# A second buffer for projected values, one key projection moved, reciprocals spread by four transfers, and another order of a store queue

## The chip, the cores and the metric

The kernel runs on 1 core of one Trainium2 chip. The metric is the device time of one execution in microseconds. A core has five engines with an instruction queue each: TensorE (PE in the profile: matmuls, with its weight loads as PEld), VectorE (DVE), ScalarE (ACT), GpSimd (POOL) and SyncE (SP). In this kernel POOL and SP compute next to nothing: POOL issues the loads, SP issues the transposing transfers, the spreads of reciprocals and the stores. Each queue is worked off in order.

## What is computed

For 8 batches, 8 heads, 1024 positions and 64 channels, attention with projected keys and values, and then a gated network over the 8192 tokens of 512 channels that come out of it:

```python
k_proj = np.einsum('ks,bhsd->bhkd', E, k)        # E, F: 64 x 1024
v_proj = np.einsum('ks,bhsd->bhkd', F, v)
scores = scale * np.matmul(q, k_proj.transpose(0, 1, 3, 2))
attn = softmax(scores)                            # over 64 projected positions
x = np.matmul(attn, v_proj)                       # rearranged to (8192, 512)
gate = 1.0 / (1.0 + np.exp(-(x @ w_gate)))        # 512 -> 1536
val = x @ w_val
out = (gate * val) @ w_out                        # 1536 -> 512
```

## The kernel before

**Work.** Matmuls are in bf16. The tokens are worked off in blocks of 512, two to a batch. A block has three units (K counts units, 3 to a block, 6 to a batch), each a third of the 1536 inner channels. The three big products are done as 2 x 2 block products with seven instead of eight multiplications: gate in `g_chain`, value in `v_chain` and output in `o_chain`; the sums of blocks that these need are made by DVE: `t_sums` (L1316, from wO to wT), `gt_sums` (from wG to gT), `xs_sums`, `s_sums`. The partial products go into PSUM banks pA0 to pA3 and pF0 to pF3, and ACT and DVE add them up, apply the sigmoid and evacuate them; `evac` (ACT, L1424) copies the output sums to the buffer ost, and SP stores them in `stored` (L1413), 4 stores of 256 KB a block. ost has four parts, and an evacuation waits for the stores that last read its parts (semaphores out0 to out3). A seed (L1653) puts a sum back into PSUM ahead of a product.

**Attention of the next batch** is interleaved with the units of the present one. In order of dependence:

- `load_k`, `load_v`, `load_q` (L395 to L430): POOL issues loads of 1 MB.
- `kv(b, bank)` (L863): 16 matmuls project keys and values into one bank. `keep_kd` (L879): ACT copies the keys to kpd, and SP issues the transfer that transposes them into kpD (L893). `vd_one` (L902): ACT copies the values into vpD, in two halves.
- `transpose_q` (L850): four transfers on SP from Qb to qT (L854).
- `sc_visit`: scores and their exponentials (eT), two visits of two rounds.
- `den_visit`: 16 matmuls with the patterns dsel8 (`den8`, L969) sum the denominators, DVE takes reciprocals (`rec`, L959) into rden; `spread` (L1126) stores rden to DRAM as rd (L1129) and reads it back with eight broadcasting transfers (L1146) into xu, seen as rb, four for each of two rounds.
- `xo_visit`: attention times values (from vpD) in a bank, and `scaled` (DVE, L1155 to L1159) multiplies it with rb into xT, the input of the next batch's gate and value products.

**Order.** The first 85 us or so are ordered by hand: a list of slots (`todo`) with pieces hung into them by `on` (L1876 to L1977). kv(2) is one of these pieces (`kv2`, L1962), together with t_sums and the transposes of q for batch 2. From there on a planner orders the work: the loop at L1997 hands it groups of matmuls with goals (times in a fictitious clock with 9.9 us per unit, PACE), and `arranged` (L52) simulates the five queues with the assumed costs in `COST` (L28; a transfer without a given time counts 3.0 us) and picks, whenever an engine is free, the ready entry with the least rank; ranks are derived backwards from goals. `Plan.add` (L146) records reads and writes by keys, and `emit` (L185) turns the result into one fixed program per engine with semaphore waits. So what the planner believes sets only the order within each queue; what an instruction really waits for follows from the keys and that order.

```python
pick = min((t for t in some if t.at <= first + 1e-9), key=lambda t: (t.rank, t.n))
...
self.busy, self.lat = (0.85 if eng == "POOL" else 0.6), t if t is not None else 3.0
```

In the loop, for a batch b the next batch's scores come in units late_ and late_+1 (late_ is 1 for b = 1, else 0), the denominators with the second of these, the first xo visit in unit late_+3, the second, and kv(b+2) after it, in unit late_+4.

Of the kernel before, what the change touches and what calls it, by code (L numbers as in the profile page):

```python
# [12 lines left out]
P = 128  # L13
# [17 lines left out]
class Task:  # L31
    def __init__(self, eng, call, t):
        self.eng, self.calls, self.goal = eng, [] if call is None else [call], None
        busy, tail = COST[eng]
        self.busy = busy if t is None else t
        self.lat = self.busy + tail
        self.dma = call is not None and call[5] is not None
        if self.dma:
            self.busy, self.lat = (0.85 if eng == "POOL" else 0.6), t if t is not None else 3.0
# [4 lines left out]
    def keys(self):  # L44
        r, w = set(), set()
        for c in self.calls:
            r.update(c[2])
            w.update(c[3] + c[4])
        return r - w, w, (r & w)


def arranged(tasks, free):  # L52
# [3 lines left out]
    for n, t in enumerate(tasks):  # L56
# [3 lines left out]
        def dep(o, raw):  # L60
# [4 lines left out]
            t.pre[o.n] = max(t.pre.get(o.n, 0.0), wait)  # L65
# [50 lines left out]
class Plan:  # L116
# [11 lines left out]
    def note(self, eng, call, t):  # L128
# [3 lines left out]
        else:  # L132
            self.tasks.append(Task(eng, call, t))

# [11 lines left out]
    def add(self, eng, fn, r=(), w=(), x=(), dma=None, t=None):  # L146
        if self.tasks is not None:
            self.note(eng, (eng, fn, tuple(r), tuple(w), tuple(x), dma), t)
            return None
# [80 lines left out]
def bass_linformer_attn__then__ffn_glu_sigmoid_kernel(  # L230
# [18 lines left out]
    with contextlib.ExitStack() as es:  # L249
# [11 lines left out]
        def within(shape, dtype):  # L261
# [24 lines left out]
        rhl = within([P, 256], BF16)  # L286
        quad = sbuf("quad", [P, 1], FP32)
        row_f = sbuf("row_f", [P, 1], FP32)
        rows = sbuf("rows", [P, 4, 32], FP32)
        half = sbuf("half", [P, 2], FP32)  # L290
        ident = sbuf("ident", [P, P], BF16)
# [10 lines left out]
        vpD = sbuf("vpD", [P, H, DH], BF16)  # L302
        qT = sbuf("qT", [P, H, 512], BF16)
        eT = sbuf("eT", [P, 8, 512], BF16)
        rden = sbuf("rden", [P, 256], FP32)
# [16 lines left out]
            "p (j h r c) -> p j h r c", j=4, h=2, r=2  # L322
        )

# [158 lines left out]

        def constants():
# [11 lines left out]
            for i, n in ((1, 8), (2, 4)):  # L496
                dve(
                    lambda e, i=i, n=n: e.tensor_copy(
                        pats[:, i, :].rearrange("p (a b) -> p a b", b=n),
                        count[:, 0:n].unsqueeze(1).to_broadcast([P, 32 // n, n]),  # L500
                    ),
                    ["count"],
                    ["pats"],
                )
# [41 lines left out]
            for t, k, m, w in ((dsel8, "dsel8", 8, 4),):  # L546
                for n in range(2):
                    for i in range(w):
                        dve(
                            lambda e, t=t, m=m, n=n, i=i: e.tensor_scalar(  # L550
                                t[:, n, i, :].rearrange("p (a b) -> p a b", b=m),
                                count[:, 0:m].unsqueeze(1).to_broadcast([P, 32 // m, m]),
                                half[:, n : n + 1],
                                2.0 * i,
                                op0=ALU.subtract,
                                op1=ALU.is_equal,
                            ),
                            ["count", ("half", n)],
                            [(k, n)],
                        )  # L560
# [77 lines left out]
        def keep_v(bks, c0, engines, R=None):  # L638
            vv = vpD[:, :, :].rearrange("p (r h) d -> p r h d", h=2)
            width = 256 if R is None else 128  # L640
            for n, (h, g) in enumerate(((0, 0), (1, 1), (0, 1), (1, 0))):
# [4 lines left out]
                ws = [("vpD", h, g, x) for x in both(R)]  # L646
# [28 lines left out]
        def VPD(R):  # L675
            return [("vpD", h, g, R) for h in range(2) for g in range(2)]
# [173 lines left out]
        def transpose_q():  # L850
            for r in range(NR):
# [8 lines left out]
                    dma=f"qT{r}",  # L860
                )
# [40 lines left out]
        def vd_one(bk, g):  # L902
            act(
                vpD[64 * g : 64 * g + 64, :, :].rearrange("p h d -> p (h d)"),
                bank[bk][64:128, :],
                [],
                [("vpD", h, g, R) for h in range(2) for R in range(2)],
# [4 lines left out]
        group = plan.group  # L912

        def attention(b):
# [44 lines left out]
            def rec(c):  # L959
                cc, bk = slice(c * P, (c + 1) * P), den_bank[0]  # L960
                dve(
                    lambda e: e.reciprocal(rden[:, cc], bank[bk][:, cc]),
                    [],
                    [("rden", c, R) for R in range(2)],
# [57 lines left out]
            def xo_one(r, bks):  # L1022
                for g in range(2):
                    n = 2 * r + g
                    for c in range(2):
# [4 lines left out]
                            vpD[kk, 2 * r + c, :],  # L1030
                            eT[kk, n, :],
                            VPD(r // 2) + [("eT", n)],
# [93 lines left out]
            def spread():  # L1126
                add(
                    "SP",
                    lambda e: e.dma_start(rd_v[b], rden[:, :]),  # L1129
                    r=[("rden", c, R) for c in range(2) for R in range(2)],  # L1130
                    w=[("rd", b)] + ([("xu", n) for n in range(8)] if b == 2 else []),
                    dma="rd",
                    t=2.8,
                )
                for rnd in range(2):
                    for c in range(2):
                        for h in range(2):
                            row = 4 * h + 2 * rnd + c
                            src = (
                                rd_v[b]  # L1140
                                .rearrange("(j m) (o c) -> o j m c", j=4, o=1)[:, :, row, :]
                                .to_broadcast([64, 4, 256])
                            )
                            add(
                                "SP",
                                lambda e, src=src, rnd=rnd, c=c, h=h: e.dma_start(  # L1146
                                    rb[64 * c : 64 * c + 64, :, h, rnd, :], src
                                ),
                                r=[("rd", b)],
                                w=[("rb", c, rnd, h)],  # L1150
                                dma=f"rb{c}{rnd}{h}",
                                t=4.0,
                            )

            def scaled(r, g, bk):  # L1155
# [6 lines left out]
                        rb[:, j, :, rnd, :],  # L1162
                        ALU.mult,
                    ),
                    [("rb", c, rnd, h) for c in range(2) for h in range(2)],
# [20 lines left out]
            def den_visit(goal, bk):  # L1186
# [14 lines left out]
                spread_keys=[("rb", c, rnd, h) for c in range(2) for rnd in range(2) for h in range(2)],  # L1201
# [75 lines left out]
        def oproj(blk, tt, pb, cols=((0, DM),)):  # L1277
# [3 lines left out]
            for n, (c0, c1) in enumerate(cols):  # L1281
                if n:
                    pb = FF.take()
                for m in range(NF):
# [5 lines left out]
                        [("hT", blk % 2, m, tt // 2), "wO"],  # L1290
# [25 lines left out]
        def t_sums(n):  # L1316
# [4 lines left out]
                3: (T3, B22, B12, ALU.subtract, ["wO"], [("wT", 3)]),  # L1321
                2: (T2, T3, B11, ALU.add, ["wO", ("wT", 3)], [("wT", 2)]),
                4: (T4, B21, T2, ALU.subtract, ["wO", ("wT", 2)], [("wT", 4)]),
                1: (B12, B12, B11, ALU.subtract, [], ["wO", ("wT", 1)]),
# [223 lines left out]
        def gt_sums(n, part=None):  # L1548
# [14 lines left out]
            w = [("gT", n, j) for j in js]  # L1563
            if n == 1:
# [297 lines left out]
        def second_loads():  # L1862
# [7 lines left out]
                ["wO"],  # L1870
# [87 lines left out]
        on(3, 2, lambda: t_sums(3))  # L1958
        on(3, 3, lambda: n1["bc"](1))
        on(3, 3, lambda: t_sums(2))  # L1960

        def kv2():  # L1962
            bk = AA.take()
            kv(2, bk)
            keep_kd(bk)
            vd_one(bk, 0)
            vd_one(bk, 1)
            AA.append(bk)

        on(3, 4, kv2)  # L1970
        on(3, 4, lambda: (t_sums(4), t_sums(1)))
        on(3, 4, transpose_q)
# [13 lines left out]

        for n in (3, 2, 4):
            gt_sums(n)
        gt_sums(1)
        for n in (1, 2, 3, 4):  # L1990
            xs_sums(2, n)
        o_chain(1, OA, OC, 0.0, 2.0, sums=False)
# [4 lines left out]
        for b in range(1, B):  # L1997
# [5 lines left out]
            for u in range(6):  # L2003
                K = 6 * b + u
                t0 = when(K)
                if n is not None:
                    if u == late_:
                        n["sc_visit"](t0 - 1.0, (0, 1), (GA, GC, XA, XB))
                    if u == late_ + 1:
                        n["sc_visit"](t0 - 1.0, (2, 3), (GA, GC, XA, XB))  # L2010
                        n["den_visit"](t0 + 6.0, XA)
                        if b + 2 < B:
                            transpose_q()
                        if b + 3 < B:
                            load_q(b + 3, n["spread_keys"])
                    if u == late_ + 3:
                        n["xo_visit"](t0 - 1.0, (0, 1), (GA, GC, XA, XB))
                    if u == late_ + 4:
# [3 lines left out]
                    if u == late_ + 4 and b + 2 < B:  # L2022
                        with group(t0 + 5.0, 1.83):
# [50 lines left out]
```

## Time and profile before

| what | value |
|---|---|
| median of 3 runs | 537.67 us (537.11 to 538.55) |
| the profiled execution's own time | 538.83 us |
| its span | 537.0 us |
| mean granted clock of TensorE | 0.983 |
| busy: PE, DVE, ACT, POOL | 508.6, 405.2, 352.0, 36.9 us |
| matmuls | 4668 |
| bytes read and written in HBM | 72.88 and 17.56 MB |

The profile's page has a busy time, a share of the span and a count for each engine, a strip of 40 slices of 13.4 us whose digits are busy tenths (PEclk: the granted clock in tenths), and the costliest groups of instructions. Asked further, the trace gives the waits (engine, line, what it waited for: total us, times, longest), the windows (busy time of each engine in a stretch of time, with the granted clock, the share of the DMA engines' time and GB/s), a timeline of a queue, and the packets of each DMA queue in a window (q0 carries POOL's loads, q1 SP's transfers). Times of transfers as SP's rows show them are of their issue; the landing is later. Matmuls of 256 columns take 0.109 us each when they stand back to back at full clock. Landings in this trace: a kpD transpose 3.2 us after its issue when alone, 9.0 in the median and 10.0 at most beside loads; the eight transfers of a spread 5.6 to 9.2 each in the steady part, the first round 9.5 us after the first issue and all at 14.1.

### The profile page before, as it was taken

The page shows a single profiled execution, that of the slowest core. Times are in us where ns is not written, and L with a number is a line of the kernel's source. Part 1 is how long each engine was busy: PE and PEld are TensorE (multiplying, and loading weights), DVE is VectorE, ACT ScalarE, POOL GpSimd, SP SyncE. Part 2 cuts the span into 40 slices and gives each one's busy share as a digit, 9 for nine tenths or more (in the row PEclk, how much of TensorE's full clock was granted, in tenths as well). Part 3 has the DMA queues.
Part 4 walks back from the last instruction along what each step waited for, and adds up shares of the span by engine and source line. Part 5 has one row for each costly group of instructions (what it writes and reads, how often), then busy time and mean ns, then how long its engine had stood idle before and what let it go on. Part 6 is the DMA issues. An engine that isn't in the chain of part 4 may idle for free.

```text
span 537.0 us, 11363 instructions
## 1 busy us (share of the span) xinstructions
PE 508.6 (95%) x4668; PEld 401.6 (75%) x4677; DVE 405.2 (75%) x670; ACT 352.0 (66%) x644; POOL 36.9 (7%) x52
## 2 busy tenths in 40 slices
PE   5999998996788999999999999999999999999996
PEld 4544544884666887888788887888788888888885
DVE  3648689674675879696978879696978879786874
ACT  2555663874365856887678856887678857676752
POOL 9310200100010001000010001000000000000000
PEclk9999998999698999999999999999999999999999
DMA  9999999898969297995969395966502090101113
GB/s 162 199 199 202 149 210 176 138 188 180 139 101 188 50 193 163 149 176 98 201 98 214 56 227 83 184 141 113 134 12 79 24 222 3 51 30 40 40 41 118
DMA packets 90692, 69.42 MB, mean 129 GB/s; under 512 B 35472, under 2 KB 82832, under 8 KB 90640
## 3 DMA queue, kind: packets, MB, share of 16 engines
q0 software_dynamic: 33984, 29.89, 36.8%
q1 hardware_dynamic: 56656, 38.81, 32.9%
q8 instruction: 36, 0.59, 0.5%
q14 instruction: 16, 0.13, 0.1%
HBM read 72.88 MB, written 17.56 MB: 168 GB/s over the span
## 4 chain that ended last, share of the span: by engine, by line
PE 88%; DMA 5%; DVE 3%; ACT 1%; issue 1%; POOL 1%; SPq 0%; DVEq 0%; ACTq 0%; POOLq 0%
PE pA L372 49%; PE pF L372 39%; DMA KVs<-in_v_dram 2%; DMA kpD<-kpd 2%; DMA xu<-rd 1%; DVE vsnap L1664 1%; DVE hT L1786 0%; DVE xT L800 0%; ACT kpd L376 0%; DVE hT L1264 0%; ACT vpD L376 0%; SPq L1146 0%; DVE hS L1345 0%; POOL KVs L390 0%; POOL Qb L390 0%
## 5 line engine op out<-in xcount | busy, mean ns | idle before, releaser
L376 ACT ACTIVATE sig<-pA 128x512 f32<-128x512 f32 x126 | 74.9, 595 | 51.2 <-PE pA L372 51.2
L1653 ACT ACTIVATE pF<-pA 128x512 f32<-128x512 f32 x99 | 58.0, 587 | 43.0 <-PE pA L372 29.9
L1664 DVE TENSOR_TENSOR vsnap<-pF,vsnap 128x512 f32<-128x512 f32 x90 | 62.0, 689 | 29.4 <-ACT vsnap L376 13.9
L1740 DVE TENSOR_TENSOR sig<-pF,sig 128x512 f32<-128x512 f32 x84 | 57.5, 684 | 23.1 <-PE pF L372 17.6
L372 PE MATMUL pF<-wO,hT 128*128 128x256 bf16 (+1 forms) x400 | 59.3, 286 | 0.2 <-issue 0.2
L1786 DVE SCALAR_TENSOR_TENSOR hT<-sig,vsnap 128x512 bf16<-128x512 f32 x84 | 57.2, 686 | 1.3
L376 ACT ACTIVATE sig<-sig 128x512 f32<-128x512 f32 x84 | 52.8, 630 | 7.8 <-DVE sig L1740 7.0
L372 PE MATMUL pF<-xS,wV 128*128 128x256 bf16 x360 | 55.0, 276 | 0.3
L376 ACT ACTIVATE vsnap<-pA 128x512 f32<-128x512 f32 x84 | 50.0, 595 | 7.4 <-PE pA L372 7.2
L372 PE MATMUL pA<-xT,vT 128*128 128x256 bf16 x336 | 51.0, 275 | 0.0
L372 PE MATMUL pF<-xT,wG 128*128 128x256 bf16 (+1 forms) x257 | 49.3, 312 | 1.5 <-DVE hT L1264 0.8
L372 PE MATMUL pA<-xT,gT 128*128 128x256 bf16 x336 | 50.5, 273 | 0.0
L372 PE MATMUL pF<-xS,wG 128*128 128x256 bf16 x336 | 50.4, 273 | 0.0
L376 ACT ACTIVATE sig<-pF 128x512 f32<-128x512 f32 x66 | 39.3, 596 | 14.9 <-PE pF L372 12.9
L372 PE MATMUL pA<-wT,hT 128*128 128x256 bf16 x360 | 48.8, 273 | 0.0
L372 PEld LDWEIGHTS pF<-wO,hT 128*128 128x128 bf16 x402 | 38.6, 98 | 10.9 <-issue 1.0
L372 PEld LDWEIGHTS pF<-xS,wV 128*128 128x128 bf16 x360 | 34.4, 99 | 10.7 <-issue 2.3
L372 PE MATMUL pF<-xT,wV 128*128 128x256 bf16 (+1 forms) x240 | 41.5, 294 | 0.0
L372 PEld LDWEIGHTS pA<-xT,vT 128*128 128x128 bf16 x336 | 31.6, 98 | 9.1 <-ACT sig L376 4.1
L372 PEld LDWEIGHTS pA<-wT,hT 128*128 128x128 bf16 x360 | 35.0, 98 | 4.6 <-issue 0.4
L1786 DVE SCALAR_TENSOR_TENSOR hT<-sig,pF 128x512 bf16<-128x512 f32 x42 | 28.6, 681 | 10.8 <-PE pF L372 10.6
L372 PEld LDWEIGHTS pF<-xS,wG 128*128 128x128 bf16 x336 | 32.9, 98 | 3.8
(150 smaller groups left out, 876.1 us busy)
## 6 DMA issues: line engine op xcount, KB each, us to landing
out_dram<-ost SPq DMA_DIRECT2D x61, 256.0 KB, 3.8
xu<-rd SPq DMA_DIRECT2D x48, 256.0 KB, 7.6
Qb<-in_q_dram POOLq DMA_DIRECT2D x7, 1024.0 KB, 9.3
KVs<-in_k_dram POOLq DMA_DIRECT2D x7, 1024.0 KB, 11.2
KVs<-in_v_dram POOLq DMA_DIRECT2D x7, 1024.0 KB, 16.0
wO<-in_moe_w_out_dram POOLq DMA_DIRECT2D x1, 1536.0 KB, 13.1
wG<-in_moe_w_gate_dram POOLq DMA_DIRECT2D x5, 256.0 KB, 18.2
wV<-in_moe_w_val_dram POOLq DMA_DIRECT2D x5, 256.0 KB, 18.8
```

The source lines that it names most:

```text
L372: return add("PE", lambda e: e.matmul(o, lhsT, rhs, **kw), r=r, x=[("bank", b)])
L376: return add("ACT", lambda e: e.activation(o, i, func, scale=scale), r=r, w=w, x=x, t=t)
L1653: lambda e: e.activation(bank[c][:, :], bank[a][:, :], AF.Copy, scale=1.0),
L1664: lambda e: e.tensor_tensor(o, bank[bk][:, :], o, ALU.add),
L1740: dve(lambda e: e.tensor_tensor(o, bank[bk][:, :], o, ALU.add), [key], [key], b=bk)
L1786: lambda e: e.scalar_tensor_tensor(o, sg.rearrange("p (j c) -> p j c", j=2), 1.0, x.rearrange("p (j c) -> p j c", j=2), ALU.add, ALU.mult,),
```

## The change

- **Two buffers of projected values.** vpD becomes vpDs with two buffers; batch b uses number (b-1) % 2.
- **kv(2)** leaves the hand-written slot and becomes part of the planned work, with its goal at -2.0, and so does everything that stood with it: the transposes of q for batch 2 and all four t_sums. It uses bank pA3 instead of pA2. A new key wO12 names the quarter of wO that t_sums(1) overwrites, so that products with the other quarters do not wait for it.
- **kv of later batches.** `next_kv` holds kv, keep_kd and the two vd_one. For b > 1 it stands before the first xo visit, with a goal 5 us ahead of that unit, instead of after the second; for b = 1 after the first xo visit. The denominators' goal is 3.0 instead of 6.0 into the unit.
- **Reciprocals.** From batch 2 on they are written to a part of xu (rdr) instead of rden. The rows of the denominators are rearranged (the patterns dsel8 and pats, through `heads8`) so that the spread takes four transfers of [64, 8, 256] (512 KB each) instead of eight of [64, 4, 256] (256 KB each); rb has its axes in another order. rden, rows and ident now lie in gT's memory.
- **Order of SP's queue.** In the planner alone, inputs of SP's entries count 3.0 us later (`pad`), except those of the spread, and the transposes of q are ordered behind the spread (`tie`). No instruction waits for anything more by that.

In the resulting program of SP, a batch from the fourth on has: the store rd, four spreads, kpD, four transposes of q, and then four stores of a block; and at the boundary to the planned part: four transposes of q, then kpD. POOL issues v(b+3) ahead of q and k; v(3) right behind kv(2).

```diff
+            t.pre[o.n] = max(t.pre.get(o.n, 0.0), wait + t.pad)
...
+            self.tasks[-1].tie = tie
+            self.tasks[-1].pad = pad if eng == "SP" else 0.0
...
+        early[0], used[0] = gT[:, :, :, :].rearrange("p a b c -> p (a b c)"), 0
+        rden = within([P, 256], FP32)
+        rows = within([P, 4, 32], FP32)
+        ident = within([P, P], BF16)
...
-        vpD = sbuf("vpD", [P, H, DH], BF16)
+        vpDs = [sbuf(f"vpD{i}", [P, H, DH], BF16) for i in range(2)]
+        vpD = vpDs[0]
...
+        rdr = xu[:, 7, 0:256]
...
-                    lambda e: e.dma_start(rd_v[b], rden[:, :]),
-                    r=[("rden", c, R) for c in range(2) for R in range(2)],
-                    w=[("rd", b)] + ([("xu", n) for n in range(8)] if b == 2 else []),
+                    lambda e: e.dma_start(rd_v[b], rdr),
+                    r=[("rdr", c) for c in range(2)],
+                    w=[("rd", b)],
...
-                        for h in range(2):
-                            row = 4 * h + 2 * rnd + c
...
+                            .rearrange("(g m) (o c) -> o g m c", g=8, o=1)[:, :, 2 * rnd + c, :]
+                            .to_broadcast([64, 8, 256])
...
-                1: (B12, B12, B11, ALU.subtract, [], ["wO", ("wT", 1)]),
+                1: (B12, B12, B11, ALU.subtract, ["wO"], ["wO12", ("wT", 1)]),
...
-        on(3, 4, kv2)
-        on(3, 4, lambda: (t_sums(4), t_sums(1)))
-        on(3, 4, transpose_q)
...
+        def next_kv(b, goal):
+            with group(goal, 1.83):
+                kv(b, XA)
+            keep_kd(XA)
+            vd_one(XA, 0, (b - 1) % 2)
+            vd_one(XA, 1, (b - 1) % 2)
...
+        next_kv(2, -2.0)
+        transpose_q()
+        t_sums(4)
+        t_sums(1)
...
-                        n["den_visit"](t0 + 6.0, XA)
+                        n["den_visit"](t0 + 3.0, XA)
                         if b + 2 < B:
-                            transpose_q()
+                            transpose_q(n["spread_keys"])
...
+                        if b > 1 and b + 2 < B:
+                            next_kv(b + 2, t0 - 5.0)
                         n["xo_visit"](t0 - 1.0, (0, 1), (GA, GC, XA, XB))
+                        if b == 1:
+                            next_kv(3, t0 + 4.0)
...
-                    if u == late_ + 4 and b + 2 < B:
-                        with group(t0 + 5.0, 1.83):
-                            kv(b + 2, XA)
-                        keep_kd(XA)
-                        vd_one(XA, 0)
-                        vd_one(XA, 1)
```

## The prediction

> **What bounds the kernel now.** I read the page's first two parts first, for the engine that carries the span and where it does not.
>
> ```profile
> PE 508.6 (95%) x4668; PEld 401.6 (75%) x4677; DVE 405.2 (75%) x670; ACT 352.0 (66%) x644; POOL 36.9 (7%) x52
> PE   5999998996788999999999999999999999999996
> PEclk9999998999698999999999999999999999999999
> ```
>
> TensorE (PE) is busy for 95%, and from slice 14 (about 175 us) to the last but one it is full at full clock. VectorE (DVE) at 75% and ScalarE (ACT) at 66% have room. What can be gained without fewer matmuls lies in the slices that show 6, 7 or 8, or a lowered clock. Second, the waits, sorted by engine, gave the stalls of PE:
>
> ```profile
> PE pA L372 <- DVE xT L1159: 8.3, 1, 8.3
> PE pA L372 <- DMA kpD<-kpd: 4.0, 1, 4.0
> PE pA L372 <- ACT vpD L376: 2.5, 1, 2.5
> ```
>
> Each happens once (the middle number). Third, the windows view around them; the columns are the window, its length, busy time of PE, PEld, DVE, ACT and POOL, granted PE clock, DMA share and GB/s:
>
> ```profile
> 88.00:92.00 4.00, 3.26 (x17) 2.31 (x18) 4.00 (x8) 1.17 (x2) 0.00 (x0) 0.57 0.91 95
> 136.00:140.00 4.00, 2.79 (x14) 1.94 (x15) 3.54 (x6) 0.58 (x1) 0.00 (x0) 0.50 1.33 198
> 164.00:168.00 4.00, 4.00 (x29) 2.60 (x22) 1.19 (x3) 2.20 (x5) 0.00 (x0) 0.63 1.20 247
> 220.00:240.00 20.00, 20.00 (x189) 16.68 (x187) 17.22 (x29) 16.00 (x30) 0.00 (x0) 1.00 1.10 182
> ```
>
> After each stall the clock is 0.50 to 0.63 for some microseconds; in the steady part (last row) PE is busy for 20.00 of 20. So a stall costs its idle time and a cold stretch behind it, which I took as the time of the matmuls after it less their time in the steady part.
>
> - 86.28 to 88.74: idle 2.46, and 16 matmuls that take 0.109 each when warm took 3.24: 1.50 more.
> - 128.95 to 137.21: idle 8.26, cold 2.84.
> - 159.63 to 163.62: idle 3.99, cold 1.57.
>
> Together 20.62 us. That is all the change can win, as it removes no matmul and the steady part has no idle time.
>
> Last, the timeline of SP's queue, which issues transposes, spreads and stores in order (start, duration, line, tensors):
>
> ```profile
> 87.39 1.22 SPq L893 DMA_TRANSPOSE kpD<-kpd  x1
> 89.34 6.83 SPq L854 DMA_TRANSPOSE qT<-Qb  x4
> 120.58 1.23 SPq L854 DMA_TRANSPOSE qT<-Qb  x1
> 121.86 0.58 SPq L1129 DMA_DIRECT2D rd<-rden  x1
> 122.54 2.62 SPq L854 DMA_TRANSPOSE qT<-Qb  x2
> 125.20 1.07 SPq L1418 DMA_DIRECT2D out_dram<-ost  x2
> 126.32 6.07 SPq L1146 DMA_DIRECT2D xu<-rd  x8
> ```
>
> **Stall 1, two vpD and the planned kv(2).** PE waited there for ACT's copies out of the bank of kv(2). In the changed kernel the product behind kv(2) uses another bank and another key of wO, so it waits for nothing: 2.46 and 1.50 go. What is late next is kpD(2). Before, SP issued it at 87.39, ahead of the four transposes of q; in the changed order it stands behind them. They wait for the load of Qb, which lands at 89.34 in this trace whatever SP does, and take 6.83 to issue, so kpD cannot be issued before 96.17. PE reaches the first score matmul of batch 2 after 10.5 us of product groups (7 of 6 matmuls at 0.655, 13 of 4 at 0.436, 0.25 of small waits), at 86.28 + 10.5 = 96.8 instead of 99.6. POOL's queue also changes: v(3) no longer stands behind k(3) (issued at 98.88) and goes out at 86.3, its packets from about 88.8, beside the transposes. In one microsecond where a load and a transpose ran together the two queues moved 139 and 138 packets (rounded to 145 over several such); alone a load moves about 205 per us and transposes 784 in one (I use 770). So v(3) has some 590 of its 1039 packets left at 91, when the transposes' packets start; both move 590 by 95.1; the 4019 left of the transposes (4 x 1024 + 512) take 5.2 more, to 100.3. A kpD transpose alone lands in 3.2, of which 0.7 is packets; half of the rest behind the last packet gives 101.6. PE is idle for 4.8, with 1.8 cold (interpolated between the second and third stall): **+6.6**. From below: v(3) costs nothing, kpD lands at 96.17 + 3.2 = 99.4, idle 2.6 and 1.5 cold: +4.1. From above: the issue slips by the 2.4 by which one transpose took longer in a crowded queue (4.08 at 132.48 against 1.71), and kpD lands in the longest time seen beside loads, 10.0: 108.6, idle 11.8, cold 2.8: +14.6.
>
> **Stall 2, the reciprocals of batch 2.** The last multiply of a round (scaled, L1155) needs the spread. In the trace rec ended at 118.15, but the store rd stood on SP behind a transpose until 121.86 (3.7), and the first spread DMA came 4.46 after it, where in the steady part it is 2.46 (2.0). In the changed order nothing stands between rec, rd and the spread, and the sums of the denominators come 1.9 earlier after the scores (14.05 against 15.95, counted in matmul groups). That is 7.6 of 8.26. Four DMAs for eight move the same 2048 packets of 1 KB, and 207 such packets passed in one us, so I give the smaller number of DMAs nothing in transfer; issuing fewer saves SP at most half of 5.62, while the packets end later than that anyway. The round lands 9.5 to 10.2 after the first issue either way: 0 to 0.7 is left, I take **0.4**, too short to cool the clock.
>
> **Stall 3, kpD(3).** kv(3) now comes 14.6 us ahead of the scores that use it, instead of 7.9. Its landing took 8.8 beside two loads; 6.7 more of lead covers the 3.99. Cost 0; if it falls behind another transpose at its longest, 2.9.
>
> **The other batches: stores behind transposes.** Here the trace of before has no stall to show, and this decides the sum. In batches 3 to 5 SP's order was rd, spread, the stores of a block, with the transposes elsewhere:
>
> ```profile
> 244.35 0.33 SPq L1129 DMA_DIRECT2D rd<-rden  x1
> 246.81 5.62 SPq L1146 DMA_DIRECT2D xu<-rd  x8
> 255.34 4.40 SPq L1418 DMA_DIRECT2D out_dram<-ost  x4
> ```
>
> Now it is rd, four spreads, kpD, four transposes of q, and only then the stores. The next block's first evacuation (ACT, ost) waits until two stores have landed, and the seed of a product stands behind it on ACT, for which PE waits. From rd's issue, R: the spread's packets are done at R + 14.7 (2.46 + 12.2). Alone, kpD and the q transposes (4608 packets) end at R + 20.7, and the first two stores land 3.6 later, at R + 24.3. PE's groups in the changed order, from the sums of the denominators (2.7 before R in the trace) to the product that uses the seed, take 30.7, so it is asked for at R + 28.0; evacuation (0.60) and seed (0.59) with 0.2 between leave R + 26.6. So uncontended it costs nothing. But v(b+3) is now loaded right behind kv(b+2), which was moved before the xo visits: it ends 12.7 after those sums, and the packets start 2.5 after the issue, at R + 12.5. Then 455 spread packets are left, which at 145 take 3.1, to R + 15.6; 584 load packets remain, shared with transposes until R + 19.7; 4024 transposes follow, to R + 24.9; two stores land at R + 28.5. PE waits 1.9. A stall of 2.46 cost 1.50 cold; for one of 1.9 I take 0.6, between 0 and 1.5. **2.5 in each of three batches, 7.5.** From below 0. From above: if a transpose among loads takes as kpD does there (9.0 median against 3.2 alone, 5.8 more) and the spread 0.9 more, the stores land at R + 31.0: idle 4.4, cold 1.6, 6.0 each, 18.
>
> The Trainium skill, page "TensorE: Matmul & The Clock Gate", section "What's actually happening", has the clock halved only after an idle window of about 3.4 us. The trace differs: 2.46 us idle was followed by a clock of 0.57. By the page the three short stalls would leave the clock alone, and the sum would be an estimated 1.8 lower.
>
> Planner-only fields (tie, pad), the rearranged patterns (same number of instructions on DVE) and rden in the memory of gT cost nothing: DVE has 3 of 20 us idle in its fullest window to hide one late instruction; without that cover one costs its 0.69.
>
> **The sum**, on the profiled execution (538.83; span 537.0): 538.83 - 20.62 + 6.6 + 0.4 + 7.5 = 532.7. That execution is 1.16 above the median of the three runs, 537.67, so **531.5**.
>
> **Rivals.**
> - *The stores are in time* (v is hidden in the idle DMA): no 7.5, 524.0. For it: 1.9 is small against what I interpolate. Against it: the packet sharing is seen in several windows. 0.27. If kpD(2) too costs only its lower bound, 521.5 and a little less: 0.06 of its own, for 521.5 or below.
> - *Slower: the stores land late by much.* One mechanism, the wait of ACT's evacuation behind transposes that share with v. It decides from (20.62 - 6.6 - 0.4) / 3 = 4.5 us per batch; at 6.0 the time is 542.0. For it: kpD's 9.0 beside loads. Against it: there it stood beside two loads, here one. 0.20, of which 0.17 is above 539.3.
> - *The change does not do what it says*: the spread of batch 2 is still held, because the same 2048 packets are shared with v(4) and the round lands at the time of all packets, 14.1 after the first issue instead of 9.5. It costs 4.6 and 1.6 cold: 537.7. 0.12.
> - *Forecast*, 526 to 536: 0.35.
>
> Chances by a bound of 0.3% (1.6 us, about what a measurement of this kernel can tell from no change): faster, below 536.1: 0.35 + 0.27 + 0.06 = 0.68, less 0.03 for the forecast's edge, plus 0.02 of the third rival: 0.67. Slower, above 539.3: 0.17 and 0.03 of the third rival: 0.20. Same: 0.13. The range, 521 to 543, leaves out 0.05 below and 0.12 above.
>
> **What would show it.** Right: PE's waits name kpD once, near 97 to 102, and no ACT vpD; SP's timeline has rd within 1 us of rec; ACT waits before ost for a DMA of out_dram in three batches, with PE idle about 2 each. Wrong: no PE idle after 170 us (first rival); a granted clock below 0.9 in three windows past 200 us (second); a wait for xT of over 2 us near 130 (third).

## The result, and the profile after

The changed kernel takes 566.38 us in the median of 4 runs (562.34 to 568.53), the kernel before 537.39 in its 4; the ratio is 1.0534, with a 95% interval of 1.0462 to 1.0607. The forecast was 531.5 with a range to 543: the change is slower, by more than the rival that had it slower. The profiled execution took 564.84, its span is 563.1.

The page of the changed kernel, the same lines as before:

```profile
PE 513.1 (91%) x4668; PEld 402.9 (72%) x4677; DVE 405.3 (72%) x670; ACT 351.5 (62%) x644; POOL 37.0 (7%) x52
PE   5999998798999969999299992999989999999996
PEclk9999999799999989999599997899989999999999
```

The dip of 6, 7, 8, 8 in slices 10 to 13 is filled; a 7 in slice 8 has come ahead of it. But in what was the steady part there are now a 6 and two 2s, the 2s with a clock of 5 to 8 beside or behind them. The waits of the changed kernel (total us, times, longest) name them:

```profile
ACT ost L382 <- DMA out_dram<-ost: 37.0, 4, 13.4
PE pA L378 <- ACT pF L1678: 29.2, 4, 11.4
PE pA L378 <- DMA kpD<-kpd: 5.8, 1, 5.8
PE pA L378 <- DVE xT L1182: 1.9, 1, 1.9
```

Read the first two together: ACT's evacuation (ost) waits for stores to land, and PE waits for the seed (pF) that stands behind it on ACT. The chain of the changed kernel shows it for the longest stall (start and duration):

```profile
273.47 3.02 DMA out_dram<-ost
276.57 0.04 ACT ost L382
277.06 0.60 ACT pF L1678
277.71 1.03 PE pA L378 x4
```

The four stalls of PE behind the seed are 4.6, 11.4, 11.0 and 2.2, one each in batches 3 to 6. Together the three PE lines are 36.9 idle, where the three stalls of before were 14.8: 22.1 more. PE's busy time, the same matmuls, is 4.5 longer (513.1 against 508.6), with a mean granted clock of 0.967 against 0.983: the clock is low behind the stalls. 22.1 and 4.5 make 26.6; the span grew by 26.1.

SP's timeline of the changed kernel around the spread of batch 4, and POOL's load in the same stretch:

```profile
238.07 0.33 SPq L1149 DMA_DIRECT2D rd<-xu  x1
239.78 5.16 SPq L1165 DMA_DIRECT2D xu<-rd  x4
249.16 4.43 SPq L910 DMA_TRANSPOSE kpD<-kpd  x1
253.69 18.12 SPq L870 DMA_TRANSPOSE qT<-Qb  x4
271.91 28.34 SPq L1441 DMA_DIRECT2D out_dram<-ost  x8
```

```profile
248.57 0.87 POOL L396 DMA_DIRECT2D KVs<-in_v_dram  x1 [46.44 <-PE pF L378]
```

In the kernel before, the first store went out 11 us after rd (244.35 to 255.34). Here it is 33.8 (238.07 to 271.91), behind four transposes that alone took 18.12 to issue, with the load of v beside them. PE stands still meanwhile, as the windows show (PE busy in the second column, the clock before the last two):

```profile
264.00:268.00 4.00, 2.28 (x21) 1.79 (x19) 4.00 (x7) 0.00 (x0) 0.00 (x0) 1.00 1.36 143
268.00:272.00 4.00, 0.00 (x0) 0.00 (x0) 1.25 (x2) 0.00 (x0) 0.00 (x0) 0.71 1.25 236
272.00:276.00 4.00, 0.00 (x0) 0.00 (x0) 0.00 (x0) 0.00 (x0) 1.74 (x2) 0.50 1.01 320
276.00:280.00 4.00, 2.29 (x11) 1.64 (x12) 0.00 (x0) 2.05 (x4) 0.01 (x1) 0.50 1.03 113
```

### The profile page after: what moved, and what is told of

It reads as the page before. It is cut to its first block, busy times and chain, and to the rows that moved or that the text cites. A ratio compares the mean times of both kernels' runs of the same rounds, so it can differ in the third digit from the quotient of the medians.

```text
span 563.1 us, 11315 instructions
## 1 busy us (share of the span) xinstructions
PE 513.1 (91%) x4668; PEld 402.9 (72%) x4677; DVE 405.3 (72%) x670; ACT 351.5 (62%) x644; POOL 37.0 (7%) x52
## 4 chain that ended last, share of the span: by engine, by line
PE 76%; SPq 9%; DMA 7%; DVE 3%; ACT 2%; issue 1%; POOL 1%; ACTq 0%; DVEq 0%; POOLq 0%
PE pA L378 42%; PE pF L378 34%; SPq L870 8%; DMA out_dram<-ost 2%; DMA KVs<-in_v_dram 2%; DMA xu<-rd 2%; SPq L1441 1%; ACT pF L1678 1%; DMA kpD<-kpd 1%; DVE xT L1182 0%; DVE hT L1811 0%; ACT ost L382 0%; ACT vsnap L382 0%; DVE xT L816 0%; DVE vsnap L1689 0%
## 5 line engine op out<-in xcount | busy, mean ns | idle before, releaser
L378 PE MATMUL pA<-xS,gT 128*128 128x256 bf16 x168 | 26.4, 282 | 29.2 <-ACT pF L1678 29.2
L378 PE MATMUL pA<-xT,gT 128*128 128x256 bf16 x336 | 51.9, 278 | 0.0
L378 PEld LDWEIGHTS pF<-xS,wV 128*128 128x128 bf16 x360 | 34.0, 98 | 10.8 <-issue 3.5
L378 PEld LDWEIGHTS pA<-xS,gT 128*128 128x128 bf16 x168 | 15.5, 99 | 34.0 <-ACT pF L1678 30.6
L1811 DVE SCALAR_TENSOR_TENSOR hT<-sig,pF 128x512 bf16<-128x512 f32 x42 | 28.6, 681 | 14.2 <-PE pF L378 12.4
## 6 DMA issues: line engine op xcount, KB each, us to landing
xu<-rd SPq DMA_DIRECT2D x24, 512.0 KB, 11.5
Qb<-in_q_dram POOLq DMA_DIRECT2D x7, 1024.0 KB, 11.2
```

Of the source, the lines that this page charges most:

```text
L378: return add("PE", lambda e: e.matmul(o, lhsT, rhs, **kw), r=r, x=[("bank", b)])
L1811: lambda e: e.scalar_tensor_tensor(o, sg.rearrange("p (j c) -> p j c", j=2), 1.0, x.rearrange("p (j c) -> p j c", j=2), ALU.add, ALU.mult,),
```

## The experiments

Four theories, each of which could make the stores late: **A**, they stand behind the transposes of q; **B**, the spread itself is slower; **C** and **D**, the loads are at fault: of v alone, or of k and v, because kv(b+2), now earlier, frees their buffers while the spread is under way. In runs 1 to 4, 8 to 10 and 18 PE's order of instructions is that of the changed kernel, in 11, 13 and 15 to 17 that of the kernel before, so that only transfers and what they wait for differ. Runs 5, 6, 12 and 14 share an order of their own; run 7's is another again. The change also lets the planner start DVE 1.5 us late in its simulation (`arranged(tasks, {"DVE": 1.5})`), which the list of the change leaves out; all runs built on the changed kernel keep it. Times are medians; ratios are to the kernel before on the same chip.

**Run 1: eight transfers instead of four**, all else of the change kept.

```diff
-                            .to_broadcast([64, 8, 256])
...
+                        for h in range(2):
...
+                                .to_broadcast([64, 4, 256])
...
+                                w=[("rb", c, rnd, h), ("spread", c, rnd, h)],
+                                dma=f"rb{c}{rnd}{h}",
```

> The changed kernel with the spread in eight transfers of [64, 4, 256] again; the order on every engine is that of the changed kernel, so this undoes the shape of the spread alone. Theory A (the stores stand on SP behind kpD and four transposes of q, which crawl because the load of v shares the DMA engines with them): the shape matters little, stalls of PE behind the seed stay at 4.6, 11.4, 11.0 and 2.2, time 562 to 568. Theory B (the four large transfers themselves are slow: the last of them landed 25.7 after the first issue, where eight took 14.1, and everything behind them is late by that): the spread lands at about 14, the stalls fall to about the 2 that the prediction gave, time 536 to 542.

560.29, ratio 1.0434 (1.0364 to 1.0504). The waits for stores fell from 37.0 to 30.6, kpD's rose to 8.0. B in the form "four transfers are slow" is not the main cause here; the interval overlaps that of the changed kernel.

**Run 2: stores ahead of the transposes of q**, by taking out pad and tie.

```diff
-            self.tasks[-1].pad = pad if eng == "SP" else 0.0
+            self.tasks[-1].pad = 0.0
...
-                            transpose_q(n["spread_keys"])
+                            transpose_q()
```

> The changed kernel without pad and tie: SP's order alone differs, the stores of a block stand ahead of the transposes of q (behind spread and kpD); PE, ACT, DVE and POOL keep their orders. Theory A: the four waits of ACT for a store go, 29.2 idle and some 6 cold: 528 to 534; the transposes stay slow beside v but have time. Theory B: the stores still stand behind a slow spread and kpD, and about half of the stalls stay: 545 to 555. Theory C (v's early load is what hurts, wherever the stores stand, because stores share the DMA engines with it): 550 or more.

555.36, 1.0322 (1.0278 to 1.0366). The waits for stores only fell to 22.8. A alone is refuted: with the transposes of q out of the way the stores still land late. The trace tells why it was no pure test of A: with the transposes done earlier, k too was loaded early, so that k (249.29) and v (250.16) ran beside the spread (issued from 240.50).

**Run 3: v loaded behind the transposes of q**, nothing else.

```diff
                 f"KV{n}",
+                r=turned() if b >= 3 else [],
```

> The changed kernel with the load of v ordered behind the transposes of q, as the load of k is; PE and SP keep the order of the changed kernel. Theory A: without v beside them spread and transposes end at about R + 21, the stores land by R + 25, and only the 2.2 of the batch that had no load of v stays, in each batch: 532 to 540. Theory B: the spread is slow by itself and the stalls stay over 5: 550 to 560. Theory C: all stalls go: 526 to 532.

536.83, 0.9991 (0.9960 to 1.0022): 29.6 us less than the changed kernel, from the order of one load per batch. SP's order is still that of the change. Waits of this run:

```profile
ACT ost L382 <- DMA out_dram<-ost: 11.1, 2, 5.7
PE pA L378 <- ACT pF L1679: 8.5, 3, 3.8
PE pA L378 <- DVE xT L1183: 4.5, 1, 4.5
```

The boundary's wait for kpD is gone too, though kpD still stands behind the transposes there: without v beside them they took 5.39 to issue instead of 10.82. What the stores still wait (8.5 for PE) comes without a load: they stand behind the transposes of q, and these behind a spread that is itself late (its last packet 21.0 after rd, the table further down has the others).

**Run 4: v late, stores first, kpD(2) first**: runs 2 and 3 together, and the transposes of q(2) ordered behind kpD(2).

```diff
-        transpose_q()
+        transpose_q([("kpD", 0)])
```

> The changed kernel with v late, the stores ahead of the transposes of q, and kpD(2) ahead of the four transposes at the boundary; PE's order is that of the changed kernel. Theory A: nothing is late any more in the batches, and kpD(2) lands before 97, so its 5.8 and the cold behind it go too: 519 to 525. If the boundary's wait is set by the load of Qb rather than by the queue, 2 to 3 stay there: 522 to 527. Theory B: as e2 less 7: 538 or more.

558.17, 1.0404 (1.0333 to 1.0474): a clear miss. The boundary's wait is gone, but the loads of k and v, which wait for the transposes of q, were free at once, as these had been done ahead of rd; both ran beside the spread (249.18 and 250.04), and the waits for stores were 27.3. "v late" had not made it late.

**Run 5: kv in its old place** for b > 1, the rest of the change kept.

```diff
-                        if b > 1 and b + 2 < B:
-                            next_kv(b + 2, t0 - 5.0)
...
+                        if b > 1 and b + 2 < B:
+                            next_kv(b + 2, t0 + 5.0)
```

> The changed kernel with kv(b+2) back behind the second xo visit for b > 1; all else of the change stays, kpD(2) behind the transposes too. Theory D (early kv frees the buffers of k and v, so their loads run beside the spread and everything that SP has queued behind it; before, they came some 30 us later): the waits of ACT for a store go, the boundary keeps its 5.8 and some 2 cold, the spread of batch 2 its 2: 525 to 531. Theory A (stores behind transposes are late by themselves): in this order three of a block's four stores still stand behind the transposes of q, some 2 with 0.6 cold stay in each batch: 533 to 540. Theory B (the shape of the spread): 540 or more.

553.25, 1.0272 (1.0199 to 1.0344): theory D alone falls. No load ran beside these spreads, and still ACT waited 18.6 for stores, PE 12.7. So something else was slow (see runs 11 to 17).

**Run 6: run 5 with the edits of run 4.**

> As the kernel with kv back in its old place, and besides without pad and tie (transposes of q ahead of rd, stores right behind the spread), with kpD(2) ahead of the transposes at the boundary and v(3) behind k(3). PE's order is the same. Theory D: the boundary's stall goes too; batch 2's spread, which shares with the loads of k, v and q of batch 3, costs 4.5 to 6 and 1.5 cold: 522 to 527. If the boundary is set by the load of Qb: 2 more.

535.17, 0.9965 (0.9941 to 0.9988). The stores are nearly in time (PE waits 1.9 for the seed); instead scaled waits for the spread in four places, 10.6 for PE, the longest 6.4 in batch 2, where the loads of batch 3 run beside rd and the spread. The next, 3.5 in batch 3, has no load beside it: its reciprocals were done at 171.01, but rd went out only at 176.74, behind the four transposes of q.

**Run 7: q(3) late too.**

```diff
-        load_q(3)
...
+                        if b == 1:
+                            load_q(3, n["spread_keys"][0::2])
```

> As the last one, with q(3) loaded only when round 0 of the spread of batch 2 has landed. k(3) and v(3) alone, 2 MB at about 205 packets of 1 KB per us, are through by some 110, ahead of rd at 113, so the spread of batch 2 has the DMA engines to itself and its stall falls to 0 to 1: 517 to 521. If the stall of batch 2 is set by the spread's own 9.5 and not by loads beside it, no change from the last: 522 to 527.

534.20, 0.9940 (0.9916 to 0.9964). The stall of batch 2 shrank to 2.8, but small waits between 150 and 230 took part of it back: the loads of batch 4, which follow q(3), now met the spread of batch 3 (rd at 174.03, its first spread at 180.46). One of 4.3 came up in batch 4, where two transposes of q now stand between rd (234.84) and the spread (237.99). For batch 2 the mechanism held, in part (0 to 1 was expected); what the later q(3) and the other order cost elsewhere had been left out.

**Run 8: run 4 with k and v loaded behind the whole spread of the batch before.** Early kv stays.

```diff
-                load_k(b + 2)
-                load_v(b + 2)
+                keys = n["spread_keys"] if b > 1 else []
+                load_k(b + 2, keys)
+                load_v(b + 2, keys)
```

> The kernel of the fourth run (v late, stores first, kpD(2) first; early kv kept) with the loads of k and v of batch b+2 ordered behind the whole spread of batch b. Theory D: the time of the loads, and not kv's place, is what cost; the spread has the DMA engines to itself again and the stores land in time: 522 to 528, against 558 with the loads beside the spread. Rival: kpD between spread and stores, which early kv puts there, delays the stores whatever the loads do: 535 to 550.

527.86, 0.9830 (0.9796 to 0.9865). Against run 4 only the time of two loads differs, and it is 30.3 us. The timeline of run 8, SP and then POOL:

```profile
231.98 0.33 SPq L1150 DMA_DIRECT2D rd<-xu  x1
233.70 5.88 SPq L1166 DMA_DIRECT2D xu<-rd  x4
243.07 3.93 SPq L911 DMA_TRANSPOSE kpD<-kpd  x1
247.09 4.49 SPq L1442 DMA_DIRECT2D out_dram<-ost  x4
```

```profile
255.95 0.89 POOL L396 DMA_DIRECT2D KVs<-in_k_dram  x1
```

The stores go out 15.1 after rd, the loads 8.9 after the stores. ACT's waits for stores are 0.2. The rival, that kpD between spread and stores hurts by itself, is out. Early kv is harmless once it doesn't start loads in the spread.

**Runs 9 and 10: run 8 with eight transfers, and that with q(3) late** (edits of runs 1 and 7).

> The kernel of the eighth run (early kv, late loads, stores first, kpD(2) first) with the spread in eight transfers again; all orders are the same. In the runs so far the packets of the spreads of batches 4 to 6 took 20 to 22 us with four transfers, 14 to 15 before with eight, even where no load and no transpose ran beside them; in the eighth run that was hidden except in batch 2 (6.5 idle) and once 1.2. If the shape is the reason: spreads back at 15, the 1.2 gone, batch 2 some 2 to 3 better: 522 to 526. If not: 527 to 529, and the spreads stay at 20 or more.

> As the last one, with q(3) loaded when round 0 of the spread of batch 2 has landed, so that rd(2) and this spread share with no load: rd lands in 2 to 3 instead of 6.7 us, and the 6.5 idle and some 3 cold of batch 2 fall to 0 to 2: 517 to 522. Against it: q(3) and its transposes come later by some 30 us, and if they collide with the spread of batch 3, 2 to 4 come back there: 521 to 525.

526.71, 0.9808 (0.9784 to 0.9832), and 527.94, 0.9830 (0.9795 to 0.9864). Run 9 has one stall left, 6.5 in batch 2, but its spreads took 18 to 20, not 15: the shape was not the whole reason for their slowness. In run 10 the stall of batch 2 fell to 2.4, and 1.5 and 2.8 came up around the spread of batch 3 (until 162.5 and 198.7), both behind waits of ACT for stores.

**Run 11: the kernel before with four transfers**, that is with the rows of the denominators and the axes of rb rearranged as well, and nothing else.

> The kernel before with the spread in four transfers (rows of the denominators rearranged, rb's axes reordered) and nothing else of the change; PE's order is that of before, SP's too but for one transpose of q that goes out ahead of rd(2). Theory B: the spreads of batches 4 to 6 take 20 to 22 instead of 15; round 0 then lands some 3 later against a margin of 3.9, and the stores behind it 6 later: 537 to 543. Rival (the slow spread comes from where the reciprocals lie or from other traffic, not from the shape): spreads at 15, 536 to 539, batch 2 perhaps 1 to 2 later through the transpose.

549.53, 1.0241 (1.0198 to 1.0284): more than expected. **Run 12: run 5 with eight transfers.**

> The kernel of the fifth run (kv of later batches in its old place, all else of the change kept) with the spread in eight transfers; all orders are the same. The fifth run was at 553 although no load ran beside the spreads. If the four-transfer shape is the reason (its spreads took 20 to 21 with the transposes of q and three stores behind them), the waits of ACT for a store shrink from 18.6 to under 5: 534 to 542. If it is the order of the stores alone, no change: 548 to 554.

539.34, 1.0046 (1.0028 to 1.0064), 13.9 less than run 5. So where transposes and stores stand right behind the spread, four transfers do cost.

**Runs 13 and 15: the kernel before with eight transfers of [32, 8, 256], and with eight of [64, 4, 256], both with rearranged rows and axes.**

> The kernel before with eight transfers of [32, 8, 256]: as many transfers and packets as before, but each reads eight rows of rd for 32 partitions instead of four rows for 64. Orders as before. If eight rows in one transfer are what makes the spread slow: as with four transfers, 20 us and 545 to 552. If the size or the number of transfers does it: spreads at 15, 536 to 539.

> The control to the four-transfer run on the kernel before: the rearranged rows and axes, but eight transfers of [64, 4, 256]. Orders as before. If only the shape of the transfers counts: spreads at 15 and 536 to 539. If the rearranged rows or axes do (rows of rd at other addresses, other places in xu): 545 to 552.

545.80, 1.0166 (1.0144 to 1.0188), and 547.43, 1.0193 (1.0168 to 1.0218). The first seemed to say "eight rows in a transfer"; its control, run 15, has four rows in each, as many transfers as before and the same sizes, and is as slow. It is the arrangement.

**Run 14: run 6 with eight transfers.**

> The kernel of the sixth run (kv in its old place, stores right behind the spread, kpD(2) first, v late) with eight transfers. If early kv brings nothing by itself: as the ninth run, 524 to 528, with the stall of batch 2 (6.5) as the only one left. If early kv hides something (kpD(3) ahead of batch 3's scores): the ninth run stays 1 to 4 faster.

528.41, 0.9842 (0.9817 to 0.9866). Beside run 9 the intervals overlap: early kv brings some 1.7 us, if anything.

**Runs 16 and 17: the kernel before with one half of the arrangement each.** Run 16 takes the axes of rb (where in xu a row lands), run 17 the rows (which of rd's rows a transfer reads):

```diff
 # run 16
-            "p (j h r c) -> p j h r c", j=4, h=2, r=2
+            "p (r j h c) -> p r j h c", j=4, h=2, r=2
 # run 17, with the patterns dsel8 and pats to it
-  .rearrange("(j m) (o c) -> o j m c", j=4, o=1)[:, :, 4 * h + 2 * rnd + c, :]
+  .rearrange("(j h m) (o c) -> o j h m c", j=4, h=2, o=1)[:, :, h, 2 * rnd + c, :]
```

> The kernel before with rb's axes in the new order (the four pieces that a transfer writes in a partition lie 2 KB apart instead of 4 KB) and nothing else; rows and transfers as before, orders as before. In the control run the spreads of batches 4 to 6 had half their packets done 10.7 to 11.9 after the first, against 8.5 to 9.4 before. If the places written in xu are the reason: about 11 again and 545 to 549. If the rows read in DRAM are: 8.5 to 9.4 and 536 to 539.

> The other half of the control: rows of the denominators rearranged (the two transfers of a round for one half of the partitions read rows 16 KB apart instead of 4 KB), axes of rb and transfers as before. If the rows are the reason: half done at about 11 and 545 to 549; if the axes: 536 to 539. If each does a part: both runs between.

537.91, 1.0004 (0.9979 to 1.0029), and 549.15, 1.0212 (1.0155 to 1.0270). The rows alone are the reason. The windows, each from about 3 us after the first spread of batch 4 was issued (first fence: kernel before, issued 246.81; second: run 17, issued 250.98; the last number is GB/s):

```profile
250.00:254.00 4.00, 4.00 (x39) 3.53 (x37) 2.27 (x4) 2.79 (x6) 0.00 (x0) 1.00 1.05 198
```

```profile
254.00:258.00 4.00, 4.00 (x39) 3.50 (x38) 2.10 (x4) 2.79 (x6) 0.00 (x0) 1.00 0.63 68
258.00:262.00 4.00, 3.72 (x36) 2.55 (x34) 1.28 (x2) 2.37 (x5) 0.00 (x0) 1.00 1.03 196
```

No other transfer of weight runs in either, and the packets of the whole spread are as many and as large. Run 17 loses the first 4 us of this stretch to 68 GB/s and then runs at the usual rate. In these 4 us a packet takes 151 ns in the mean, against 86 in the kernel before, and the share of the DMA engines' time is 0.63 against 1.05. Its waits:

```profile
DVE xT L1170 <- DMA xu<-rd: 19.7, 4, 10.6
PE pA L372 <- DVE xT L1170: 16.0, 5, 10.1
```

Run 16 has only the old stall of batch 2 there, 8.4. The packet records of the traces, counted from the first packet of rd, give the time by which half of a spread's packets were done, for batches 4, 5 and 6:

| kernel | half of the spread done, us |
|---|---|
| before | 9.4, 8.6, 8.5 |
| run 16, axes | 9.9, 8.6, 8.6 |
| run 17, rows | 12.4, 11.4, 11.0 |
| run 15, rows and axes, eight | 11.9, 11.0, 10.7 |
| run 11, rows and axes, four | 13.1, 11.9, 11.4 |
| changed | 11.7, 11.5, 10.8 |

**Run 18: run 9 with rows and axes as before.**

> The kernel of the ninth run (526.7) with rows and axes as before; eight transfers, orders the same. The arrangement cost some 2.3 us in the first half of a spread; only the spread of batch 2 still has a stall there (6.5 idle and some 3 cold), so it should fall to about 4 idle: 522 to 525. If that spread is set by the loads beside it alone: 526 to 527.

524.21, 0.9760 (0.9725 to 0.9796): faster than both kernels. The spreads are back (8.7, 8.9, 8.5), and the stall of batch 2 is the only one left:

```profile
PE pA L378 <- DVE xT L1173: 4.2, 1, 4.2
ACT ost L382 <- DMA out_dram<-ost: 0.3, 1, 0.3
```

It holds of the change: two vpD, the planned kv(2), early kv, reciprocals in xu. It drops four transfers, rows and axes, pad and tie, and adds the late loads and kpD(2) first.

## Why the prediction was wrong

- **What bounds the kernel** was read rightly: the wait for vpD and kpD(3)'s are gone from PE's list, and batch 2's went from 8.3 to 1.9. In run 18, with the loads kept out of the spreads, nothing but 4.2 idle is left of the 14.8.
- **Stall 1, kpD(2) at the boundary.** Forecast: landing at 101.6, 4.8 idle. Measured: issued at 99.20, landed 2.83 later at 102.0, 5.8 idle. The mechanism, transposes sharing with v, holds: run 3 took away v alone, and the wait was gone (run 4 took away v and the order). The lower bound, 4.1 with v free of cost, was wrong: in run 3, with kpD still last, it was issued at 93.25, not 96.17, and landed at 96.1, ahead of the first score product at 96.20.
- **Stall 2.** Forecast 0.4, from a round's landing of 9.5 to 10.2; measured 1.9. The landing that ended the wait came at 134.55, 12.1 after the first issue (122.42): the same slower spread. Once the boundary's stall is gone, a second thing that the working left out sets this place: rd and the spread meet the loads of batch 3. In run 8 rd at 113.33 was followed by the first spread only at 120.03, and PE waited 6.5.
- **Stall 3.** Forecast 0, measured none.
- **"I give the smaller number of DMAs nothing in transfer"** and **"the rearranged patterns ... cost nothing".** This failed first. As many packets of the same size were taken for the same time. The rows alone cost the kernel before 11.2 us (run 17), with four transfers 12.3 (run 11).
- **"2.5 in each of three batches, 7.5."** The mechanism was right and the size wrong: 29.2 idle in four batches. The step that failed is the end of the spread. In batch 4 (R, the issue of rd, is 238.07) the working had its packets done at R + 15.6; the last one ended at R + 24.6 (262.7), 9.0 later. From there to the stores the working had 12.9, measured are 13.8: the store that ACT waited for landed at R + 38.4 (276.50), not R + 28.5. PE asked when it was forecast to, at R + 28.2, so the 9.9 went through to it: 1.9 and 9.9 make 11.8, measured 11.4.
- Most of the 9.9 is there without v. In run 3 the last packet of this spread ends at R + 21.0 and the stores land at R + 30.8, where the working without a load had R + 14.7 and R + 24.3. Batch 6 of the changed kernel, which has no load of v, still waited 2.2. The load of v then moved the stores by 7.7, for which the working had 4.2.
- The 14.7 was also misread: the 12.2 in it runs from the spread's first packet, which came 1.4 after the first issue. In the trace of before the last packet of that spread ends at R + 16.1.
- What made the spread late in that place is not one cause. The time from R to its last packet, with one thing more in each row, and several in the last:

| kernel | batch 4, us | batch 5, us |
|---|---|---|
| run 18: old rows, eight transfers, late loads | 15.4 | 16.0 |
| run 9: the new rows and axes | 20.4 | 19.9 |
| run 8: four transfers | 21.9 | 22.2 |
| changed: v beside the spread, transposes ahead of the stores | 24.6 | 24.1 |

- The rows are the largest part of the late spread, 4 to 5 us (the axes alone did nothing in run 16). In the time of the whole kernel the parts do not add up: with all of the change but the load of v it is 536.8; with all but four transfers 560.3; with late loads, the other order of SP and eight transfers, the rows are worth only 2.5 (run 9 against 18, whose intervals just overlap). A late transfer costs nothing until it has used up the slack of the wait, 2.3 for the stores by the prediction's working.
- **The rivals.** The slower one named the right place, ACT's evacuation behind transposes beside v, and 6.0 per batch; two batches had 11. Its upper bound took the longest rows that the trace of before had, where no spread, load and transposes had ever stood together. The rule on the clock that was weighed would have made the sum smaller, away from the result.

The Trainium skill, page "DMA: Bandwidth & Descriptors", section "Queues, rings and completion order", says that a copy is split over rings of up to 16 engines, that each engine works its ring in order, and that it takes turns between queues. The traces agree: in run 17, 365 packets of stores had started before the last packet of batch 4's spread, the first of them 4.2 us before it, so by that reading some engines were done with the spread well before others. The first store, issued at 261.43, still landed only at 270.5, behind that last packet (269.3). So in that run the tail of the spread, and not its mean rate, set when the stores landed.

What stays open: why these rows are read more slowly. A round's two transfers for one half of the partitions read rows 16 KB apart instead of 4 KB; that the memory behind serves such rows worse was not measured by itself, though in the slow stretch the single packets took longer. Nor is it clear why the last batch's spread shows little of it (half done at 8.5 in run 17, 7.9 before), and batch 3's in the changed kernel too (8.9; 9.2 before, 7.6 in run 18).

## What to carry to other kernels

When an edit lets a buffer go earlier, ask which load is waiting for it and what that load will run beside; here one load per batch, moved by its buffer and by no line that names it, cost 30 us. A transfer with the same packets is not the same transfer if its addresses change: time it alone, with the rest of the kernel as it was. And where a queue holds a chain of transfers ahead of the one that matters, bound its end by rows in which all of them run at once, or take the bound as unknown.

## What the runs showed of the hardware that was not expected

- Reading reciprocals back in the same eight transfers and 2048 packets of 1 KB ran at 68 GB/s instead of 198 for some 4 us when the rows read were others (run 17 against the kernel before).
- Four transposes of 256 KB took 18.12 us to issue behind a spread and beside a load, 5.39 at the boundary of run 3 with neither.
- One load of 1 MB per batch, issued into a spread or after the transposes, moved the end of the kernel by 29.6 us (the changed kernel against run 3), though the projection that reads it came far later in both (landing at 270.0 and projection at 320.8 in the changed kernel, 276.1 and 301.9 in run 3).
